# Attention pieces moved to a fixed table of FFN half slots, score steps in pairs, and another order of loads at the start

## The chip, the cores and the metric

The kernel runs on one core of a Trainium2 chip. The metric is the time of one execution on the device in microseconds (us). The engines are TensorE (PE in the profile), VectorE (DVE), ScalarE (ACT), GpSimd (POOL) and SyncE (SP), which here only issues transfers. Each engine works through its own queue in order and waits for others by semaphores.

## The reference, cut to what matters

Attention with a decay over 8 batches of 8 heads, 576 positions, 64 columns; its output x is normalised and goes through a gated FFN (512 to 1536 to 512) over all 4608 rows:

```python
scores = scale * q @ k.T;  cum = cumsum(log(clip(f, 1e-4, 1)))
attn = softmax(where(causal, -1e9, scores + cum[:, None] - cum[None, :]))
x = (attn @ v)                        # -> 4608 x 512, rows by batch and position
xn = x / sqrt(mean(x * x) + 1e-6) * rms_g
out = (silu(xn @ w_gate) * (xn @ w_val)) @ w_out
```

## The kernel before, in words

**Attention.** A batch has four pairs of heads, p = 0 to 3. For a pair, `cast` (L169) brings q and k to bf16; `transposes` (L192) turns the nine 128 x 128 blocks of q and k in two parts through the one PSUM bank `tr`, and VectorE copies each part to QK (L202). `scores` (L241) makes three steps, bank 0 to 2, each in a buffer `bg`; ScalarE takes the exponential of 128 x 1024 (L248) and GpSimd sets the masked triangle to zero (L216). `scores4` (L221) is the small step for the last 64 keys, in the bank `po`. `values` (L266), once a head, multiplies with the scaled v (`scale_v`, L177, on GpSimd), and VectorE divides by the row sums into x (L277, L278). `po` is one bank, so each head waits until the x of the head before it is out.

**Between.** `squares` (L288), `root` (L294, L296, GpSimd), `normed` (L305) and `transpose_x` (L307) make the normalised x and turn it, again through `tr`, to xT (L318). The rows of one batch lie in two FFN groups, since a batch has 576 rows and a group 512.

**FFN.** Nine groups. A group has 32 half slots h: 0 to 23 are `gate` (even) and `value` (odd) of the 12 chunks of 128 columns, 24 to 31 the two halves of the four projections. A gate takes a `bg` buffer; ScalarE makes a tanh of it (L387), VectorE combines (L388), the value goes to the other half of the same buffer, and VectorE makes hT (L396). A projection's result is copied out by ScalarE to `ores` (L411). `bg` has three buffers, shared by gates, projections and score steps, handed out in turn: each waits for the last reader of the third buffer before it.

**The order.** Every engine's order is that in which the program calls these functions. Batch 0 goes first, alone (L436 to L459). From batch 1 on the pieces of attention form a list of steps (`attention`, `finish`, `first`), and `knots` (L470) spreads the list evenly over the half slots, so that batch g + 1 ends within group g. Transfers of q, k and v are issued on SP's queue, those of batch 0's v and of the weights on GpSimd's.

Of the kernel before, what the change touches and what calls it, by code (L numbers as in the profile page):

```python
# [9 lines left out]
BF16 = mybir.dt.bfloat16  # L10
# [12 lines left out]
def kernel(  # L23
# [30 lines left out]
    qkt = ctx.enter_context(tc.tile_pool(name="qkt", bufs=2))  # L54
# [31 lines left out]
    def load_pair(n, what="qkv"):  # L86

        b, h0, i = n // NP, 2 * (n % NP), n % NST
        for name, src, dst in (("q", q, q32[i]), ("k", k, k32[i]), ("v", v, v32[i])):
            for h in range(2 * (name in what)):  # L90
                eng = nc.gpsimd if name == "v" and b == 0 else nc.sync
                eng.dma_start(out=dst[:, h, :, :], in_=src[b, h0 + h, 0:512, :].rearrange("(j p) d -> p j d", p=128))  # L92

    def load_last(b, what="qkv"):
        for name, src, dst in (("q", q, r32[b % 2][0:64, :, :]), ("k", k, r32[b % 2][64:128, :, :]), ("v", v, s32[b % 2])):
            if name in what:
                eng = nc.gpsimd if name == "v" and b == 0 else nc.sync
# [209 lines left out]
    def transpose_x(b, dc):  # L307
        xn = xns[b]
        tp = ps_tr.tile([128, NB * 128], BF16, name="tr")
        for j in range(NB):  # L310
            nc.tensor.transpose(tp[:, j * 128:(j + 1) * 128], xn[:, j, dc * 128:(dc + 1) * 128], ident)  # L311
        t0 = b * S
        while t0 < (b + 1) * S:
            g = t0 // GT
            t1 = min((g + 1) * GT, (b + 1) * S)
            if g not in xTs:
                xTs[g] = xtp.tile([128, NDC, GT], BF16, name="xT")
            nc.vector.tensor_scalar_mul(xTs[g][:, dc, t0 - g * GT:t1 - g * GT],  # L318
                                        tp[:, t0 - b * S:t1 - b * S], rg[:, dc:dc + 1])
            t0 = t1  # L320

    def attention(b):


        def tr(p, part):
            return lambda: transposes(b, p, part)

        def sc(p, bank):
            return lambda: scores(b, p, bank)

        def val(h):
            return lambda: values(b, h)

        def ahead(p):
            return lambda: (cast(b, p), scale_v(b, p)) if p < NP else None

        a = []
        for p in range(NP):
            a += [[tr(p + 1, 0)] if p + 1 < NP else [],
                  [sc(p, 0)],  # L340
                  [val(2 * p - 2), ahead(p + 2)] if p else [ahead(2)],
                  [tr(p + 1, 1)] if p + 1 < NP else [],
                  [sc(p, 1)],
                  [val(2 * p - 1)] if p else [],
                  [lambda p=p: scores4(b, p)],
                  [sc(p, 2)],
                  []]
        return a

    def finish(b):  # L350

        def sq(*js):
            return [lambda j=j: squares(b, j) for j in js]

        def xn(*js):
            return [lambda j=j: normed(b, j) for j in js]

        def x(dc):
            return [lambda: transpose_x(b, dc)]

        return {2: [lambda: values(b, 6)], 5: [lambda: values(b, 7)], 6: sq(0, 1), 7: sq(2, 3),
                8: sq(4) + [lambda: root(b)], 10: xn(0, 1), 11: xn(2, 3), 12: xn(4),
                14: x(0), 16: x(1), 18: x(2), 20: x(3)}

    def first(b):

        return {0: [lambda: (cast(b, 0), scale_v(b, 0))], 3: [lambda: (cast(b, 1), scale_v(b, 1))],
                5: [lambda: transposes(b, 0, 0)], 8: [lambda: transposes(b, 0, 1)]}
# [54 lines left out]
    def merged(*parts):  # L423

        n = max(at + (max(p) + 1 if isinstance(p, dict) else len(p)) for at, p in parts)
        a = [[] for _ in range(n)]
        for at, p in parts:
            for i, work in (p.items() if isinstance(p, dict) else enumerate(p)):
                a[at + i] += work
        return a  # L430

    def run(works):
        for work in works:
            work()

    def order():  # L436
# [33 lines left out]
        knots = [(0, 0), (2, 0)] + [(per * g, 9 + n * g + 21) for g in range(1, B)]  # L470
        assert knots[-1][1] == len(stream), (knots, len(stream))
        i = 0
        for h, work in enumerate(ffn):
            if h == 4:
# [3 lines left out]
            for (h0, i0), (h1, i1) in zip(knots, knots[1:]):
                if h0 <= h < h1:
                    want = i0 + (i1 - i0) * (h - h0) / (h1 - h0)  # L480
                    while i < want:
                        run(stream[i])
                        i += 1
            if h >= knots[-1][0]:
                while i < len(stream):
                    run(stream[i])
                    i += 1
            work()
# [34 lines left out]
```

## Time and profile before

| | us |
|---|---|
| median of two timed runs | 470.27 (470.17 to 470.38) |
| profiled execution | 470.79, span 468.8 |
| TensorE busy | 400.8 (85%) |
| VectorE, ScalarE, GpSimd busy | 262.3, 214.1, 179.1 |
| mean granted TensorE clock | 0.97 of 2.4 GHz |
| first FFN group's first matmul | 58.2 after the span's start |
| first group; five equal groups; group 6; group 7 | 64.25; 48.13 each; 39.72; 31.08 |

Times of rows are counted from the span's start. A matmul's end is modelled and overlaps the next one, so the distance from one start to the next tells more than a listed duration. An idle time stands in brackets with what ended it.

### The profile page before, as it was taken

The numbers are of one execution on the slowest core, as the hardware profiler recorded it, in microseconds if no ns is written. First come the engines' busy times: TensorE is split into PE (matmuls) and PEld (weight loads), VectorE is DVE, ScalarE is ACT, GpSimd is POOL, SyncE is SP. The second block draws the span as 40 slices with busy tenths as digits, with TensorE's granted clock in tenths as the row PEclk, the third lists the DMA queues.
The fourth block names the chain that finished last, engine by engine and source line by source line (L and its number), as shares of the span: only waits on it lengthen the run. The fifth ranks groups of instructions, "written<-read, shape, count | busy, mean of one in ns | idle before, by whom it ended". The sixth has DMA issues, their size and how long they took to land.

```text
span 468.8 us, 8739 instructions
## 1 busy us (share of the span) xinstructions
PE 400.8 (85%) x3317; PEld 201.1 (43%) x3317; DVE 262.3 (56%) x544; ACT 214.1 (46%) x354; POOL 179.1 (38%) x362
## 2 busy tenths in 40 slices
PE   0385398986999899989998999899989998999996
PEld 0153144543444444444444544444444444444442
DVE  1742565734575646674766377627762775572670
ACT  1354226654547435644554455535563543332321
POOL 6383718665173517351735173516451111000000
PEclk9996589998999999999999999999999999999999
DMA  9999498993173416431553146320001000101002
GB/s 159 210 200 204 107 179 146 181 199 96 45 156 83 110 48 138 102 92 67 128 111 90 68 107 130 75 85 2 2 24 45 24 1 28 62 1 69 22 1 89
DMA packets 120298, 43.19 MB, mean 92 GB/s; under 512 B 110688, under 2 KB 115296, under 8 KB 120256
## 3 DMA queue, kind: packets, MB, share of 16 engines
q1 hardware_dynamic: 115088, 36.73, 34.8%
q0 software_dynamic: 5168, 5.90, 7.5%
q8 instruction: 26, 0.43, 0.4%
q14 instruction: 16, 0.13, 0.1%
HBM read 37.90 MB, written 9.44 MB: 101 GB/s over the span
## 4 chain that ended last, share of the span: by engine, by line
PE 63%; DVE 17%; ACT 6%; POOL 4%; issue 4%; SPq 3%; DMA 2%; POOLq 0%; DVEq 0%; ACTq 0%
PE bg L384 16%; PE bg L405 16%; PE bg L394 15%; PE po L274 5%; PE bg L212 4%; DVE xn L305 4%; DVE th L388 3%; DVE x L278 3%; SPq L92 3%; ACT th L387 3%; DVE hT L396 2%; PE tr L311 2%; PE tr L200 2%; ACT junk L288 2%; DVE QK L202 2%
## 5 line engine op out<-in xcount | busy, mean ns | idle before, releaser
L388 DVE SCALAR_TENSOR_TENSOR th<-th,bg 128x512 f32<-128x512 f32 x108 | 74.2, 687 | 81.6 <-ACT th L387 81.4
L248 ACT ACTIVATE PT<-bg 128x1024 bf16<-128x1024 f32 x96 | 97.8, 1022 | 47.7 <-PE bg L212 47.3
L387 ACT ACTIVATE th<-bg 128x512 f32<-128x512 f32 x108 | 64.4, 596 | 106.1 <-PE bg L384 103.7
L384 PE MATMUL bg<-xT,wg 128*128 128x512 bf16 x432 | 112.2, 383 | 0.0
L394 PE MATMUL bg<-xT,wv 128*128 128x512 bf16 x432 | 112.1, 382 | 0.0
L405 PE MATMUL bg<-wo,hT 128*128 128x512 bf16 x432 | 102.3, 383 | 2.0 <-DVE hT L396 2.0
L216 POOL TENSOR_SCALAR_AFFINE_SELECT PT<-PT 128x256 bf16<-128x256 bf16 (+1 forms) x96 | 47.6, 495 | 92.3 <-ACT PT L248 91.2
L396 DVE SCALAR_TENSOR_TENSOR hT<-th,bg 128x512 bf16<-128x512 f32 x108 | 74.0, 685 | 10.3 <-PE bg L394 2.3
L405 PEld LDWEIGHTS <-hT 128*128 128x128 bf16 x432 | 39.9, 98 | 46.8 <-issue 3.6
L394 PEld LDWEIGHTS <-wv 128*128 128x128 bf16 x432 | 38.2, 98 | 42.9 <-issue 5.9
L384 PEld LDWEIGHTS <-wg 128*128 128x128 bf16 x432 | 37.8, 99 | 37.2 <-issue 1.4
L200 PE MATMUL tr<-ident,qkb 128*128 128x128 bf16 x288 | 28.8, 229 | 28.7 <-DVE QK L202 8.2
L318 DVE TENSOR_SCALAR xT<-tr,rg 128x512 bf16<-128x512 bf16 (+7 forms) x64 | 20.6, 363 | 56.3 <-PE tr L311 56.3
L411 ACT COPY ores<-bg 128x512 f32<-128x512 f32 x36 | 21.1, 585 | 55.0 <-PE bg L405 55.0
L274 PEld LDWEIGHTS <-PT 128*128 128x128 bf16 x896 | 36.6, 101 | 18.9 <-POOL PT L216 6.0
L212 PE MATMUL bg<-QK 64*128 64x64 bf16 (+3 forms) x576 | 39.9, 247 | 0.0
L200 PEld LDWEIGHTS <-qkb 128*128 128x128 bf16 x288 | 21.1, 102 | 41.6 <-issue 16.6
L202 DVE COPY QK<-tr 128x640 bf16<-128x640 bf16 x64 | 28.9, 451 | 10.9 <-PE tr L200 10.9
L311 PE MATMUL tr<-ident,xn 128*128 128x128 bf16 x160 | 16.3, 233 | 20.4 <-DVE QK L202 12.0
L278 DVE TENSOR_TENSOR x<-po,rden 128x320 f32<-128x320 f32 x64 | 31.5, 492 | 2.4 <-DVE rden L277 0.2
L212 PEld LDWEIGHTS <-QK 64*128 64x128 bf16 x576 | 17.0, 97 | 28.3 <-issue 24.3
L274 PE MATMUL po<-Vs_119,PT 128*128 128x65 bf16 x448 | 22.2, 204 | 5.1 <-POOL PT L216 3.7
(105 smaller groups left out, 296.0 us busy)
## 6 DMA issues: line engine op xcount, KB each, us to landing
out_dram<-ores SPq DMA_DIRECT2D x36, 256.0 KB, 2.0
q_0_103<-in_q_dram SPq DMA_DIRECT2D x16, 128.0 KB, 2.9
k_0_107<-in_k_dram SPq DMA_DIRECT2D x16, 128.0 KB, 3.3
q_1_104<-in_q_dram SPq DMA_DIRECT2D x16, 128.0 KB, 3.4
k_1_108<-in_k_dram SPq DMA_DIRECT2D x16, 128.0 KB, 3.5
q_2_105<-in_q_dram SPq DMA_DIRECT2D x16, 128.0 KB, 3.0
k_2_109<-in_k_dram SPq DMA_DIRECT2D x16, 128.0 KB, 3.6
q_3_106<-in_q_dram SPq DMA_DIRECT2D x16, 128.0 KB, 2.7
```

The lines of the kernel that those rows point to most:

```text
L200: nc.tensor.transpose(tp[:, (c - c0) * 128:(c - c0 + 1) * 128], src[:, c, :, :].rearrange("p h d -> p (h d)"), ident)
L212: nc.tensor.matmul(sc[:, par, c:c + n], lhsT=QK[b, p][rows, KEYS[kj]:KEYS[kj] + 128], rhs=QK[b, p][rows, q0:q0 + n], start=True, stop=True)
L216: nc.gpsimd.affine_select(out=d, in_=d, pattern=pattern, compare_op=ALU.is_ge, fill=0.0, base=0, channel_multiplier=-1)
L248: nc.scalar.activation(t, sc, ACT.Exp, scale=scale)
L274: nc.tensor.matmul(po[:, qi, :], lhsT=weights_of(b, h, qi, kj), rhs=Vs[b % 2][:, kj, h, :], start=(kj == 0), stop=(kj == qi))
L278: nc.vector.tensor_tensor(xs[b][:, :, h * D:(h + 1) * D], po[:, :, 0:D], bcast(r[:, :], D), ALU.mult)
L384: nc.tensor.matmul(pg, lhsT=wg[:, dc, fc * 128:(fc + 1) * 128], rhs=xTs[g][:, dc, :], start=(dc == 0), stop=(dc == NDC - 1))
L387: readers[g, fc] = (nc.scalar.activation(t, pg, ACT.Tanh, scale=0.5), nc.vector.scalar_tensor_tensor(t, in0=t, scalar=1.0, in1=pg, op0=ALU ...
L388: nc.vector.scalar_tensor_tensor(t, in0=t, scalar=1.0, in1=pg, op0=ALU.add, op1=ALU.mult))
L394: beside(nc.tensor.matmul(pv, lhsT=wv[:, dc, fc * 128:(fc + 1) * 128], rhs=xTs[g][:, dc, :], start=(dc == 0), stop=(dc == NDC - 1)), reade ...
L396: nc.vector.scalar_tensor_tensor(hT, in0=ths.pop((g, fc)), scalar=0.5, in1=pv, op0=ALU.mult, op1=ALU.mult)
L405: beside(nc.tensor.matmul(po, lhsT=hTs[g, fc][:, j * 128:(j + 1) * 128], rhs=wo[:, fc, :], start=(fc == 0), stop=(fc == NFC - 1)), readers ...
```

## The change

Batch 0: k and its last rows (r) go by the Pool queue, v by SP; the pieces of the four pairs stand in another order, the value step one pair behind; x is turned into two idle `bg` buffers, all four parts, and then copied out by VectorE and ScalarE in turn. QK has three buffers instead of two. The ones column of V goes from VectorE to GpSimd. From batch 1 on a table says which piece stands ahead of which half slot of a group, the same in each: `ALL1` for batch 1 beside group 0; `ONE`, a block with no FFN between, ahead of group 1; `LAST` (second half of batch g + 1) and `FIRST` (first half of batch g + 2) beside groups 1 to 8. A piece is a letter and its arguments: C cast and scale_v, T transposes, S scores, L scores4, V values, Q squares, R root, N normed, X transpose_x. Two score steps mostly stand together.

```diff
-    qkt = ctx.enter_context(tc.tile_pool(name="qkt", bufs=2))
+    qkt = ctx.enter_context(tc.tile_pool(name="qkt", bufs=3))
...
-    load_pair(0, "qk")
-    load_last(0, "qk")
-    load_pair(0, "v")
-    load_pair(1, "qk")
-    load_last(0, "v")
-    load_pair(1, "v")
-    load_pair(2)
-    load_pair(3)
+    for n in range(NP):
+        load_pair(n, "q")
+        load_pair(n, "k", nc.gpsimd)
+        if n == 0:
+            load_last(0, "q")
+            load_last(0, "k", nc.gpsimd)
+        load_pair(n, "v")
+        if n == 0:
+            load_last(0, "v")
...
-        for b in range(2):
-            nc.vector.tensor_copy(Vs[b][:, :, :, D], decT[:, :, b * H:(b + 1) * H])
+        nc.gpsimd.tensor_copy(Vs[0][:, :, :, D], decT[:, :, 0:H])
...
-    def transpose_x(b, dc):
-        xn = xns[b]
-        tp = ps_tr.tile([128, NB * 128], BF16, name="tr")
+    def turn_x(b, dc, tp):
         for j in range(NB):
-            nc.tensor.transpose(tp[:, j * 128:(j + 1) * 128], xn[:, j, dc * 128:(dc + 1) * 128], ident)
+            nc.tensor.transpose(tp[:, j * 128:(j + 1) * 128], xns[b][:, j, dc * 128:(dc + 1) * 128], ident)
+
+    def put_x(b, dc, tp, on_act=False):
+
         t0 = b * S
         while t0 < (b + 1) * S:
             g = t0 // GT
             t1 = min((g + 1) * GT, (b + 1) * S)
             if g not in xTs:
                 xTs[g] = xtp.tile([128, NDC, GT], BF16, name="xT")
-            nc.vector.tensor_scalar_mul(xTs[g][:, dc, t0 - g * GT:t1 - g * GT],
-                                        tp[:, t0 - b * S:t1 - b * S], rg[:, dc:dc + 1])
+            dst, src = xTs[g][:, dc, t0 - g * GT:t1 - g * GT], tp[:, t0 - b * S:t1 - b * S]
+            if on_act:
+                nc.scalar.mul(dst, src, rg[:, dc:dc + 1])
+            else:
+                nc.vector.tensor_scalar_mul(dst, src, rg[:, dc:dc + 1])
             t0 = t1
 
...
+    LAST = {2: "S22 S30", 4: "L2", 6: "V4", 8: "S31 S32 V5", 10: "L3", 12: "V6", 14: "V7", 15: "Q0", 16: "Q1",
...
+    FIRST = {2: "T00", 5: "T01", 11: "C1", 14: "S00 S01", 16: "T10", 17: "C2", 18: "T11", 20: "S02 S10 T20",
...
+    ALL1 = {2: "C1", 3: "T00", 4: "T01", 6: "C2", 7: "S00 S01 T10", 8: "T11", 10: "C3", 11: "S02 S10", 12: "L0 T20",
...
+    ONE = ("1N0 1N1 1N2 1N3 1N4 2T00 2T01 2S00 2S01 2T10 2T11 2S02 2S10 1X0 2L0 2T20 1X1 2S11 2S12 2V0 1X2 2T21 2V1 2L1 "
...
+        for p in range(NP):
+            scores(0, p, 0)
+            if p > 0:
+                scores4(0, p - 1)
+            if p + 1 < NP:
+                cast(0, p + 1)
+                transposes(0, p + 1, 0)
+            scores(0, p, 1)
+            if p + 1 < NP:
+                scale_v(0, p + 1)
+            if p > 0:
+                values(0, 2 * p - 2)
+            if p + 1 < NP:
+                transposes(0, p + 1, 1)
+            scores(0, p, 2)
+            if p > 0:
+                values(0, 2 * p - 1)
+            if p == 1:
+                load_last(1)
+            if p == 2:
+                load_w(0)
+        scores4(0, 3)
         values(0, 6)
         values(0, 7)
+        load_w(1)
         for j in range(NB):
             squares(0, j, nc.vector if j % 2 else None)
         root(0)
         for j in range(NB):
             normed(0, j, on_act=j % 2 == 1)
+        banks = [ps_b.tile([128, 2, 1024], BF16, name="bg") for _ in range(2)]
         for dc in range(NDC):
-            transpose_x(0, dc)
-
-        n = 9 * NP
-        parts = [(0, first(1))]
-        for b in range(1, B):
-            at = 9 + n * (b - 1)
-            parts += [(at, attention(b)), (at + n, finish(b))]
-            if b + 1 < B:
-                parts.append((at + n - 9, first(b + 1)))
-        stream = merged(*parts)
+            turn_x(0, dc, banks[dc // 2][:, dc % 2, :])
+        for dc in range(NDC):
+            put_x(0, dc, banks[dc // 2][:, dc % 2, :], on_act=dc % 2 == 1)
+        piece(1, "C0")
...
+            if g == 0:
+                for what in ALL1.get(h, "").split():
+                    piece(1, what)
+                if h in (16, 22, 27):
+                    piece(2, {16: "C0", 22: "C1", 27: "C2"}[h])
+            else:
+                if g == 1 and h == 0:
+                    for what in ONE.split():
+                        piece(int(what[0]), what[1:])
+                        if what == "2S10":
+                            piece(2, "C3")
+                for what in LAST.get(h, "").split():
+                    piece(g + 1, what)
+                for what in FIRST.get(h, "").split():
+                    piece(g + 2, what)
+                for what in NEXT.get(h, "").split():
+                    piece(g + 3, what)
+                if g == 1 and h == 0:
+                    piece(3, "C0")
             work()
```

In the order of the engines this shows at three places. First the start: SP's queue before, from its first transfer on (q_0 and k_0 are pair 0, r_0 the last 64 rows of q and k, v and s the same of v):

```order
L101 DMA fr<-in_f_dram 64x576
L92 DMA q_0_103<-in_q_dram 128x4x64 x2
L92 DMA k_0_107<-in_k_dram 128x4x64 x2
L98 DMA r_0_115<-in_q_dram 64x8x64
L98 DMA r_0_115<-in_k_dram 64x8x64
L92 DMA q_1_104<-in_q_dram 128x4x64 x2
```

and POOL's queue now, from its first transfer on:

```order
L91 DMA k_0_107<-in_k_dram 128x4x64
masks.py:199 ISA
masks.py:199 AFFINE_SELECT ident_f<-ident_f 128x128
L91 DMA k_0_107<-in_k_dram 128x4x64
L96 DMA r_0_115<-in_k_dram 64x8x64
L91 DMA k_1_108<-in_k_dram 128x4x64 x2
```

The k part of r moved from SP's fifth group of transfers to Pool's third transfer, where s of v stood before.

Second, VectorE at the end of batch 1. Before, beside the projections of group 0 (QK is the copy of turned q and k, xn the normalised x, xT its turned copy, rden and x the end of a value step):

```order
L202 COPY QK<-tr 128x640
L396 SCALAR_TENSOR_TENSOR hT<-th,bg 128x512
L277 RECIPROCAL rden<-po 128x5
L278 TENSOR_TENSOR x<-po,rden 128x5x64
L202 COPY QK<-tr 128x512
L277 RECIPROCAL rden<-po 128x5
L278 TENSOR_TENSOR x<-po,rden 128x5x64
L202 COPY QK<-tr 128x640
L305 TENSOR_SCALAR xn<-x,rs 128x512 x4
```

and now, in the block ahead of group 1:

```order
L275 RECIPROCAL rden<-po 128x5
L276 TENSOR_TENSOR x<-po,rden 128x5x64
L303 TENSOR_SCALAR xn<-x,rs 128x512 x5
L200 COPY QK<-tr 128x640
L200 COPY QK<-tr 128x512
L200 COPY QK<-tr 128x640
L200 COPY QK<-tr 128x512
L321 TENSOR_SCALAR xT<-tr,rg 128x448
L321 TENSOR_SCALAR xT<-tr,rg 128x128
```

The five xn stand ahead of the first of four QK copies in a row; before, QK copies stood between the steps that lead up to them.

Third, ScalarE in a steady group. Before (th is the tanh of a gate, PT the exponential of a score step, PT_0 to PT_2 those of the small step):

```order
L387 ACTIVATE th<-bg 128x512
L248 ACTIVATE PT<-bg 128x1024
L387 ACTIVATE th<-bg 128x512
L228 ACTIVATE PT_1_122<-po 128x2x64
L248 ACTIVATE PT<-bg 128x1024
L387 ACTIVATE th<-bg 128x512 x2
```

and now, from a group's first gate on:

```order
L346 ACTIVATE th<-bg 128x512
L246 ACTIVATE PT<-bg 128x1024 x2
L346 ACTIVATE th<-bg 128x512
L226 ACTIVATE PT_2_123<-po 128x2x64
L346 ACTIVATE th<-bg 128x512 x2
L246 ACTIVATE PT<-bg 128x1024 x2
```

One exponential between two tanh became two, with more tanh between the pairs.

## Rows read from the trace of the kernel before

**Rows 1.** Busy time of each engine by stage: start:end, length, busy (instructions), clock, DMA share.

```profile
0.00:16.00 16.00, 1.20 (x9) 0.94 (x9) 5.24 (x19) 2.67 (x3) 7.86 (x18) 1.00 1.02 174
...
58.20:122.45 64.25, 54.87 (x516) 28.05 (x515) 33.45 (x74) 32.03 (x51) 34.33 (x72) 0.94 0.78 151
...
170.58:218.72 48.14, 44.41 (x398) 22.31 (x396) 29.15 (x63) 24.86 (x42) 21.43 (x44) 1.00 0.40 97
...
363.12:402.84 39.72, 37.93 (x280) 18.21 (x279) 24.38 (x49) 17.46 (x33) 4.44 (x9) 1.00 0.08 28
402.84:433.92 31.08, 31.08 (x145) 14.07 (x144) 17.14 (x26) 9.31 (x16) 0.00 (x0) 1.00 0.09 35
```

**Rows 2.** Timeline of the start: start, duration, engine, line, operation, count [idle before].

```profile
3.50 0.70 POOL L98 DMA_DIRECT2D s_0_117<-in_v_dram  x1
...
11.81 0.23 DVE L174 CAST qkb<-r_0_115 128x128 bf16<-128x128 f32 x1 [4.99 <-DMA r_0_115<-in_k_dram]
...
18.31 0.49 DVE L161 COPY decT<-po 128x320 f32<-128x320 f32 x1 [1.60 <-PE po L160]
...
22.21 1.02 ACT L248 ACTIVATE PT<-bg 128x1024 bf16<-128x1024 f32 x1 [4.84 <-PE bg L212]
```

**Rows 3.** Transfers by issuing line: queue, count, size, median us from issue to landing.

```profile
wv<-in_moe_w_val_dram POOLq DMA_DIRECT2D x3, 512.0 KB, 10.6
...
s_0_117<-in_v_dram POOLq DMA_DIRECT2D x1, 128.0 KB, 5.7
```

**Rows 4.** Timeline of batch 0's pairs and its end.

```profile
30.89 0.61 PE L212 MATMUL bg<-QK 64*128 64x64 bf16 x10
...
47.33 0.49 DVE L278 TENSOR_TENSOR x<-po,rden 128x320 f32<-128x320 f32 x1
...
56.23 0.71 PE L311 MATMUL tr<-ident,xn 128*128 128x128 bf16 x5 [0.74 <-DVE xT L318]
...
58.19 1.91 PE L384 MATMUL bg<-xT,wg 128*128 128x512 bf16 x4
```

**Rows 5.** Timeline of TensorE in a steady group.

```profile
174.49 1.03 PE L394 MATMUL bg<-xT,wv 128*128 128x512 bf16 x4
175.44 0.40 PE L212 MATMUL bg<-QK 64*128 64x64 bf16 x10
175.78 1.04 PE L384 MATMUL bg<-xT,wg 128*128 128x512 bf16 x4
...
182.28 0.59 PE L274 MATMUL po<-Vs_120,PT 128*128 128x65 bf16 x14
...
182.74 0.44 PE L200 MATMUL tr<-ident,qkb 128*128 128x128 bf16 x5
```

**Rows 6.** Timelines of VectorE and ScalarE in the same group.

```profile
174.96 0.69 DVE L388 SCALAR_TENSOR_TENSOR th<-th,bg 128x512 f32<-128x512 f32 x1 [0.59 <-ACT th L387]
175.75 0.69 DVE L396 SCALAR_TENSOR_TENSOR hT<-th,bg 128x512 bf16<-128x512 f32 x1
...
196.93 0.62 ACT L288 ACTIVATE junk<-x 128x512 bf16<-128x512 f32 x1
...
197.67 0.63 ACT L288 ACTIVATE junk<-x 128x512 bf16<-128x512 f32 x1
...
198.30 1.00 ACT L248 ACTIVATE PT<-bg 128x1024 bf16<-128x1024 f32 x1
199.21 0.59 ACT L387 ACTIVATE th<-bg 128x512 f32<-128x512 f32 x1
...
213.46 0.58 ACT L411 COPY ores<-bg 128x512 f32<-128x512 f32 x1 [1.67 <-PE bg L405]
```

**Rows 7.** Timelines at the end of the first group.

```profile
108.98 2.17 DVE L305 TENSOR_SCALAR xn<-x,rs 128x512 bf16<-128x512 f32 x4 [3.98 <-POOL rs L296]
...
112.56 0.44 PE L311 MATMUL tr<-ident,xn 128*128 128x128 bf16 x5 [2.94 <-DVE QK L202]
```

**Rows 8.** Busy time by stretch, behind that wait.

```profile
114.00:116.00 2.00, 2.00 (x7) 0.79 (x6) 0.31 (x1) 0.00 (x0) 0.00 (x0) 0.50 0.80 180
```

More of the change, by code (lines that the diff above doesn't have):

```diff
@@ L84, with load_pair @@
     QB = [consts.tile([128, 128], BF16, name=f"QB_{i}") for i in range(3)]
-    def load_pair(n, what="qkv"):
+    def load_pair(n, what="qkv", eng=nc.sync):
         b, h0, i = n // NP, 2 * (n % NP), n % NST
@@ L178, in scale_v @@
         n, h0 = b * NP + p, 2 * p
-        if b > 1 and p == 0:
+        if b > 0 and p == 0:
             nc.gpsimd.tensor_copy(Vs[b % 2][:, :, :, D], decT[:, :, b * H:(b + 1) * H])
@@ L317, in transpose_x @@
                 xTs[g] = xtp.tile([128, NDC, GT], BF16, name="xT")
-            nc.vector.tensor_scalar_mul(xTs[g][:, dc, t0 - g * GT:t1 - g * GT],
-                                        tp[:, t0 - b * S:t1 - b * S], rg[:, dc:dc + 1])
-            t0 = t1
[L322 to L368, printed above, removed]
+            dst, src = xTs[g][:, dc, t0 - g * GT:t1 - g * GT], tp[:, t0 - b * S:t1 - b * S]
[3 more added lines that the diff above has]
+                nc.vector.tensor_scalar_mul(dst, src, rg[:, dc:dc + 1])
+            t0 = t1
+    def transpose_x(b, dc):
+        tp = ps_tr.tile([128, NB * 128], BF16, name="tr")
+        turn_x(b, dc, tp)
+        put_x(b, dc, tp)
     hTs = {}
@@ L420, with piece @@
             ffn += [lambda g=g, j=j: project(g, j, 0), lambda g=g, j=j: project(g, j, 1)]
[L423 to L434, printed above, removed]
+    def piece(b, what):
+        kind, args = what[0], [int(c) for c in what[1:]]
+        if not 0 <= b < B:
+            return
+        if kind == "C":
+            cast(b, *args)
+            scale_v(b, *args)
+        elif kind == "N":
+            normed(b, *args)
+        else:
+            {"T": transposes, "S": scores, "L": scores4, "V": values, "Q": squares, "R": root,
+             "X": transpose_x}[kind](b, *args)
+    LAST = {2: "S22 S30", 4: "L2", 6: "V4", 8: "S31 S32 V5", 10: "L3", 12: "V6", 14: "V7", 15: "Q0", 16: "Q1",
+            17: "Q2", 18: "Q3", 19: "Q4 R", 21: "N0", 22: "N1", 23: "N2", 24: "N3", 25: "N4", 26: "X0", 27: "X1",
+            29: "X2", 31: "X3"}
+    FIRST = {2: "T00", 5: "T01", 11: "C1", 14: "S00 S01", 16: "T10", 17: "C2", 18: "T11", 20: "S02 S10 T20",
+             22: "L0", 23: "T21 C3", 24: "V0", 26: "S11 S12 V1", 28: "L1 T30", 29: "V2", 30: "S20 S21 V3 T31"}
+    NEXT = {28: "C0"}
+    ALL1 = {2: "C1", 3: "T00", 4: "T01", 6: "C2", 7: "S00 S01 T10", 8: "T11", 10: "C3", 11: "S02 S10", 12: "L0 T20",
+            14: "S11 S12 V0", 15: "T21", 16: "V1", 17: "L1", 18: "S20 S21 V2", 19: "T30", 20: "V3", 21: "T31",
+            22: "L2", 23: "S22 S30", 25: "S31 S32 V4", 27: "V5", 28: "L3", 29: "V6", 30: "V7",
+            31: "Q0 Q1 Q2 Q3 Q4 R"}
+    ONE = ("1N0 1N1 1N2 1N3 1N4 2T00 2T01 2S00 2S01 2T10 2T11 2S02 2S10 1X0 2L0 2T20 1X1 2S11 2S12 2V0 1X2 2T21 2V1 2L1 "
+           "1X3 2S20 2S21 2V2 2T30 2V3 2T31")
     def order():
@@ L470, in order @@
[L470 to L474, printed above, removed]
+            turn_x(0, dc, banks[dc // 2][:, dc % 2, :])
+        for dc in range(NDC):
+            put_x(0, dc, banks[dc // 2][:, dc % 2, :], on_act=dc % 2 == 1)
+        piece(1, "C0")
+        per = 2 * (NFC + 4)
+        for i, work in enumerate(ffn):
+            g, h = i // per, i % per
+            if i == 2:
@@ L475, in order @@
                 load_w(2)
-            if h == 10:
+            if i == 9:
                 load_wo()
[L478 to L487, printed above, removed]
+            if g == 0:
[3 more added lines that the diff above has]
+                    piece(2, {16: "C0", 22: "C1", 27: "C2"}[h])
+            else:
+                if g == 1 and h == 0:
[11 more added lines that the diff above has]
+                    piece(3, "C0")
```

11 lines of the change are left out of this document (1 added, 10 removed).

## The prediction

> **What bounds the kernel now.** I read the busy time of each engine by stage first, since TensorE is the busiest in every FFN stage [rows 1], then the timelines of each stage for what TensorE waits for. In rows 1 a group of the FFN alone takes 31.08 us (144 matmuls, 0.216 each: 0.86 for a gate or value half slot, 1.30 for half a projection). Each of five equal groups, with one batch of attention beside it, takes 48.1; the first takes 64.25, the one with the end of batch 7 39.72. TensorE's first FFN matmul starts the first of these stages, at 58.2. So the span is 58.2 + 64.25 + 5 x 48.13 + 39.72 + 65.96 (two bare groups and the last transfer) = 468.8, and the change touches every term but the last. The profiled run took 470.79; the two timed runs have a median of 470.27, 0.5 less.
>
> **The start.** The first cast of batch 0 waits until 11.81 for the k part of tile r [rows 2], the fifth transfer group on SP. Now that part stands third in the Pool queue, where s stood: issued at 3.50 [rows 2], landed a median 5.7 later [rows 3], so 9.2, and 2.6 us come off. Bounds: 0 (the same 16 engines carry it all) and 5 (k could land with q). I take 2.6, since s had the same bytes ahead of it. The page DMA: Bandwidth & Descriptors of the Trainium skill (Rules for kernel authors) says that spreading transfers over queues wins no bandwidth, only issue time; by that the 2.6 would be 0, and no run here shows it yet.
>
> The first score step stood behind the cast and turn of pair 1, so the first exponential ran at 22.21. Now only the decay columns precede it: their copy at 18.31 [rows 2], less 2.6, gives 15.7, and 0.54 of scores and the handover make 16.4; so 5.8 earlier. From there to the last x (47.33 + 0.49 [rows 4]) the old loop took 25.6 for four pairs. At the lower clock a pair costs TensorE three score steps of 0.54, turns of about 0.64 and 0.54 [rows 4], two value steps of 1.0 (about twice their later 0.44) and one small step of 0.2 = 5.0; with about 0.9 of waits (the x of one head must be out of the bank before the next) I find the same 25.6 and take no gain there.
>
> In the tail x was turned through one bank, each of three turns waiting 0.74 for VectorE's copy [rows 4]. Two idle FFN banks take that wait away: 2.2. ScalarE's two copies end before the gate's last matmul needs them. First gate: 58.2 - 5.8 - 2.2 = **50.2**. The weights come in time: the first pair is asked for in pair 2's work, near 32 by this count, and lands up to 10.6 later [rows 3]; the second, asked for after the last value step near 42, is first read by the fifth gate, past 60.
>
> **A steady group.** Attention beside it costs TensorE 4 x (turns 0.28 + 0.23, three score steps of 0.33, 0.07, two value steps of 0.44) + 4 turns of x of 0.28 = 10.9 (a listed duration ends about 0.16 after the next may start) [rows 5]. Work: 42.0, so the old group loses 6.1. What the table loses, I follow by its queues. From a gate's end to its hT's end: 0.21 to the tanh, 0.63 to the first VectorE step, 0.79 to the second, 0.69 for it = 2.3 [rows 6]. A gate takes the buffer of the third last bg tile. After a pair of score steps that is the gate before, whose value (0.86) and the pair (0.66) cover 1.5 to 1.9. So the gates at half slots 2, 8, 14 and 20 wait 0.57, 0.41, 0.41 and 0.67. In the last, the five squares also stand ahead of the tanh (0.63 to 0.75 each). The third projection and the next group's first gate take a buffer whose last reader is the copy to ores, just issued: 0.21 + 0.58 + 0.05 [rows 6], less 0.35 of pieces in the first case: 0.49 and 0.85. The first turn of x waits 0.85 for the last xn, one turn 0.13. Sum 4.4. The other gates' waits are covered: each has a buffer freed two half slots earlier.
>
> A score step alone costs 0.33 and a seam ahead: the value before it takes 0.95 instead of 0.86 [rows 5]. A pair has one seam; some fall into the waits, and I charge 0.2. Group: 42.0 + 4.4 + 0.2 = **46.6**, 1.5 less, five times 7.7. The page TensorEngine Tiling (Array Packing) of the skill (Key Properties) says that a change of tiling mode drains the engine, with which the 0.09 agrees; charging all six seams by it would make 46.9.
>
> Group 6 has only batch 7's rest: 31.1 + 4.3 + waits 1.8 + 0.2 = **37.4**, 2.3 less.
>
> **The first group and the block behind it.** Here the change costs. The old 64.25 held batch 1, its x and more than half of batch 2, spread out. Now batch 1 alone lies in the first group: 31.1 + 9.8, waits of the same kinds 5.9 (eight waits of 0.2 to 0.95; the second turn, two gates and the first projection carry 3.1), 1.8 for the lower clock at the start (the old first gate took 1.91 [rows 4]): 48.6. Then xn, x and half of batch 2 run with no FFN between. Batch 1's squares start only with the last half projection. Five of 0.75 [rows 6], of which 1.2 lie beside it, the root 1.5 and five xn of 0.54 [rows 7] end 6.8 after the projection. VectorE has them ahead of its first QK copy, so TensorE gets one turn done and stands. Then eleven turns go through the one transposing bank, each with its copy about 1.1 at full clock: 12; the waits for x between value steps add 2. Together 20.7. At the lower clock turns, scores and values on this path cost about 6.5 more: 27. The old kernel shows the clock after a hole: a wait of 2.94 before 112.56 [rows 7] is followed by a granted clock of 0.50 at 114 to 116 [rows 8], that is 1.2 of 2.4 GHz. The new hole is twice as long and TensorE half idle behind it, so I take 25.8, near the slow end. First group and block: **74.4**, 10.2 more than before.
>
> **Sum.** 50.2 + 74.4 + 233.0 + 37.4 + 66.0 = 461.0 for 468.8; 7.8 off 470.79 and the 0.5: **462.5**.
>
> **Costed at nothing.** The ones column of V on GpSimd instead of VectorE lies beside pair 0's exponentials; without that cover it costs its 0.4. The third QK buffer only removes waits. GpSimd is busy 21.4 of 48.1 in a group [rows 1], so its masks and casts come in time; bunched four deep they would delay a value step by about 1.
>
> **Rivals.**
> 1. The clock stays up. If the start is dense enough to be granted 2.4 GHz early, and the block too, the block costs 20.7 and the loop at the start gives 2: 462.5 - 5.1 - 2 = 455.4. For: the pairs at the start leave TensorE about 0.9 idle in 5.9. Against: the old hole [rows 7, 8]. Chance 0.22.
> 2. The steady groups win nothing. With every queued step at its listed length (exponential 1.00, tanh 0.59, VectorE 0.69) instead of start to start (0.91, 0.47, 0.60), the same walk makes 48.0 a group: 469.5. Chance 0.14.
> 3. The Pool queue brings k no sooner: +2.6, 465.1. All queues share the 16 engines, whose share is 1.02 in the first 16 us [rows 1], so k waits among the same bytes. Against: s landed by 9.2 in that crowd. The Trainium skill's page named above states this as its rule. Chance 0.09.
> 4. Slower: ScalarE becomes the bound behind the paired score steps. Two exponentials (2 x 0.91) stand ahead of the next tanh. The walk has that tanh needed only three buffers later. If the gate that waits is one whose own tanh is behind the pair, each such place costs 1.83 per group. One place per group makes 472; two make 481, slower by over 2%. It decides from 48.2 us a group on, where the other gains are used up. For: six such pairs stand at fixed places in each group, where the old order had one exponential at a time. Against: ScalarE is busy 24.9 of 48.1 [rows 1]. Chance 0.07.
>
> **Numbers.** My forecast has 0.48, with 457 to 467 as its own range (block 20.7 to 27, group 45.9 to 47.4, start 0 to 5). Range of all: 453 to 470; it leaves out the slower rival and the tails. Two per cent, about what a measurement of this kernel can tell from no change, is 9.4 us: 460.9 and 479.7. Faster: rival 1 and the lower part of my own (0.48 x 0.42), 0.42. Slower: 0.05. Within: 0.53.
>
> **What would show it.** The first exponential near 16.4 and the r cast near 9.2; the first gate near 50; in the profile by stage the hole of about 6 us before batch 1's xn, with the clock at 0.50 behind it; gates behind pairs waiting for hT, and the first gate of each group for ores; groups of 46 to 47. A steady group over 48, or a block of 30, would make the forecast wrong; a clock of 1.00 through the block would make it too high.

## The result, and the profile after

The changed kernel takes 442.19 us (two runs, 440.19 and 444.19) for 470.27: a ratio of 0.940 (0.922 to 0.959). Timed again in more rounds, it took 442.12, 442.49, 443.90 and 444.88, ratio 0.943 (0.941 to 0.945); a fifth run, which took 591 at a mean granted clock of 0.66, is left out. The median of these four, 443.2, is what the experiments are held against. The forecast was 462.5, with 453 as its low end: wrong, the time lies below the range.

Busy time by stage, as in [rows 1], of the profiled run of 444.19 (span 442.5): start, first group, the block, a stretch of the block, a steady group, group 6.

```profile
14.00:47.66 33.66, 21.18 (x248) 14.40 (x249) 17.21 (x41) 16.89 (x26) 21.91 (x40) 0.78 1.20 202
47.66:92.66 45.00, 42.72 (x374) 21.78 (x380) 24.92 (x50) 24.41 (x40) 27.54 (x55) 0.98 1.13 203
92.66:117.98 25.32, 15.03 (x164) 10.62 (x163) 10.14 (x28) 10.60 (x17) 10.48 (x25) 0.60 0.26 72
98.00:100.00 2.00, 0.71 (x6) 0.44 (x7) 1.14 (x3) 0.00 (x0) 0.46 (x2) 0.50 0.00 0
206.35:250.63 44.28, 42.50 (x390) 22.91 (x396) 28.63 (x61) 25.10 (x42) 21.34 (x44) 1.00 0.42 105
339.57:376.35 36.78, 35.46 (x249) 17.72 (x254) 23.10 (x45) 17.09 (x32) 3.82 (x8) 1.00 0.08 30
```

Stage by stage, from the first gate of each group:

| stage | before | forecast | after | error |
|---|---|---|---|---|
| start, to the first gate | 58.2 | 50.2 | 47.7 | -2.5 |
| first group | 64.25 (with half of batch 2) | 48.6 | 45.0 | -3.6 |
| block | none | 25.8 | 25.3 | -0.5 |
| five steady groups | 240.7 | 233.0 | 221.6 | -11.4 |
| group 6 | 39.7 | 37.4 | 36.8 | -0.6 |
| rest | 66.0 | 66.0 | 66.1 | +0.1 |

The errors add to 18.5, which is the whole difference between 461.0 and 442.5, the spans forecast and profiled. Five steady groups carry 11.4 of it. The waits of TensorE in one of them, before (four waits) and after (one row, four waits); columns are total, times, longest. Before, 170.42 to 218.56:

```profile
PE tr L311 <- DVE QK L202: 1.8, 1, 1.8
PE tr L200 <- DVE xT L318: 0.8, 1, 0.8
PE tr L200 <- DVE QK L202: 0.7, 1, 0.7
PE bg L405 <- DVE hT L396: 0.2, 1, 0.2
```

After, 206.35 to 250.63:

```profile
PE bg L343 <- DVE hT L355: 1.4, 4, 0.4
```

The turns no longer stand in line; the gates behind the pairs wait for hT, at the four places forecast, but nobody waits for ores. A listed wait begins at the modelled end of the matmul before it, which reaches past the next possible start, so it is shorter than what is lost from start to start. TensorE at the fourth place, half slot 20:

```profile
225.89 0.44 PE L198 MATMUL tr<-ident,qkb 128*128 128x128 bf16 x5
226.17 1.03 PE L343 MATMUL bg<-xT,wg 128*128 128x512 bf16 x4
...
229.19 1.03 PE L353 MATMUL bg<-xT,wv 128*128 128x512 bf16 x4
230.15 0.62 PE L210 MATMUL bg<-QK 64*128 64x64 bf16 x12
230.70 0.45 PE L198 MATMUL tr<-ident,qkb 128*128 128x128 bf16 x5
231.56 1.02 PE L343 MATMUL bg<-xT,wg 128*128 128x512 bf16 x3 [0.40 <-DVE hT L355]
```

A turn of five blocks with no wait behind it takes 0.28 to the gate (225.89 to 226.17), here 0.86: the gate waits 0.58, of which 0.40 is listed. At half slots 2, 8 and 14 the same count gives 0.58, 0.40 and 0.39; in all that is 1.9 where the list has 1.35.

The end of that group and the start of the next show that nobody waits for ores. Timeline of TensorE and then of ScalarE (start, duration, idle time before in brackets), to be read with [rows 5, 6]:

```profile
249.34 1.46 PE L364 MATMUL bg<-wo,hT 128*128 128x512 bf16 x6
250.63 1.03 PE L343 MATMUL bg<-xT,wg 128*128 128x512 bf16 x3
```

```profile
247.12 1.95 ACT L246 ACTIVATE PT<-bg 128x1024 bf16<-128x1024 f32 x2
250.88 0.59 ACT L370 COPY ores<-bg 128x512 f32<-128x512 f32 x1 [1.81 <-issue]
```

The gate starts 1.29 after the projection's half, with no gap, and 0.25 before the copy to ores even begins. Of the three buffers one still waits for that copy, so the gate has one of the pair's, whose exponentials ran from 247.12 to 249.07.

The start in the same run, as in [rows 2, 4]: the r cast, the decay columns, then ScalarE's first exponential, then TensorE from the turns of x on.

```profile
9.01 0.23 DVE L172 CAST qkb<-r_0_115 128x128 bf16<-128x128 f32 x1 [2.19 <-DMA r_0_115<-in_k_dram]
...
15.51 0.49 DVE L160 COPY decT<-po 128x320 f32<-128x320 f32 x1 [1.60 <-PE po L159]
...
39.56 0.49 DVE L276 TENSOR_TENSOR x<-po,rden 128x320 f32<-128x320 f32 x1
```

```profile
15.95 1.02 ACT L246 ACTIVATE PT<-bg 128x1024 bf16<-128x1024 f32 x1 [1.38 <-PE bg L210]
```

```profile
44.80 0.83 PE L307 MATMUL bg<-ident,xn 128*128 128x128 bf16 x4 [5.51 <-DVE xn L303]
45.98 1.89 PE L307 MATMUL bg<-ident,xn 128*128 128x128 bf16 x16 [0.35 <-DVE xn L303]
47.66 2.19 PE L343 MATMUL bg<-xT,wg 128*128 128x512 bf16 x4
```

And the block's hole, which answers to [rows 7]: VectorE's xn, and behind them the QK copy on which TensorE waits for 5.79.

```profile
96.25 2.07 DVE L303 TENSOR_SCALAR xn<-x,rs 128x512 bf16<-128x512 f32 x5 [5.38 <-POOL rs L294]
98.23 0.48 DVE L200 COPY QK<-tr 128x640 bf16<-128x640 bf16 x1
```

```profile
98.77 0.58 PE L198 MATMUL tr<-ident,qkb 128*128 128x128 bf16 x4 [5.79 <-DVE QK L200]
```

### The profile page after: what moved, and what is told of

It is laid out like the page before. It is cut to its first block, busy times and chain, and to the rows that moved or that the text cites. A ratio compares the mean times of both kernels' runs of the same rounds, so it can differ in the third digit from the quotient of the medians.

```text
span 442.5 us, 8691 instructions
## 1 busy us (share of the span) xinstructions
PE 390.3 (88%) x3264; PEld 208.0 (47%) x3317; DVE 257.7 (58%) x538; ACT 217.0 (49%) x358; POOL 178.0 (40%) x364
## 4 chain that ended last, share of the span: by engine, by line
PE 78%; DVE 9%; ACT 5%; issue 4%; POOL 2%; DMA 1%; DVEq 0%; ACTq 0%; POOLq 0%
PE bg L364 20%; PE bg L343 19%; PE bg L353 18%; PE po L272 7%; PE bg L210 6%; PE tr L198 3%; DVE hT L355 3%; PE tr L307 2%; ACT PT L246 2%; DVE th L347 1%; DMA r_0_115<-in_k_dram 1%; ACT junk L286 1%; DVE x L276 1%; DVE QK L200 1%; ACT th L346 1%
## 5 line engine op out<-in xcount | busy, mean ns | idle before, releaser
L343 PE MATMUL bg<-xT,wg 128*128 128x512 bf16 x400 | 109.1, 381 | 10.3 <-DVE hT L355 8.4
L353 PE MATMUL bg<-xT,wv 128*128 128x512 bf16 x427 | 110.0, 379 | 0.3 <-issue 0.2
L246 ACT ACTIVATE PT<-bg 128x1024 bf16<-128x1024 f32 x96 | 93.6, 1022 | 33.3 <-PE bg L210 33.2
L364 PE MATMUL bg<-wo,hT 128*128 128x512 bf16 x416 | 99.0, 379 | 0.8
L353 PEld LDWEIGHTS <-wv 128*128 128x128 bf16 x432 | 41.4, 98 | 47.7 <-issue 1.2
L343 PEld LDWEIGHTS <-wg 128*128 128x128 bf16 x432 | 39.9, 98 | 47.7 <-issue 11.4
L210 PE MATMUL bg<-QK 64*128 64x64 bf16 (+3 forms) x576 | 35.4, 254 | 0.8 <-DVE QK L200 0.5
L200 DVE COPY QK<-tr 128x640 bf16<-128x640 bf16 x64 | 28.9, 451 | 11.4 <-PE tr L198 11.3
L321 DVE TENSOR_SCALAR xT<-tr,rg 128x448 bf16<-128x448 bf16 (+7 forms) x56 | 18.0, 363 | 23.8 <-PE tr L307 23.8
L275 DVE RECIPROCAL rden<-po 128x5 f32<-128x5 f32 x64 | 12.2, 190 | 32.0 <-PE po L272 32.0
L286 ACT ACTIVATE junk<-x 128x512 bf16<-128x512 f32 x38 | 23.9, 628 | 4.9 <-DVE x L276 4.4
```

Of the source, the lines that this page charges most:

```text
L210: nc.tensor.matmul(sc[:, par, c:c + n], lhsT=QK[b, p][rows, KEYS[kj]:KEYS[kj] + 128], rhs=QK[b, p][rows, q0:q0 + n], start=True, stop=True)
L246: nc.scalar.activation(t, sc, ACT.Exp, scale=scale)
L343: nc.tensor.matmul(pg, lhsT=wg[:, dc, fc * 128:(fc + 1) * 128], rhs=xTs[g][:, dc, :], start=(dc == 0), stop=(dc == NDC - 1))
L353: beside(nc.tensor.matmul(pv, lhsT=wv[:, dc, fc * 128:(fc + 1) * 128], rhs=xTs[g][:, dc, :], start=(dc == 0), stop=(dc == NDC - 1)), reade ...
L364: beside(nc.tensor.matmul(po, lhsT=hTs[g, fc][:, j * 128:(j + 1) * 128], rhs=wo[:, fc, :], start=(fc == 0), stop=(fc == NFC - 1)), readers ...
```

## The experiments

**The change again.** No edit.

> The changed kernel itself again, in more rounds. Theory (its time differs from run to run by when the clock rises in batch 0's pairs): 439 to 444, the first gate at 46 to 47.7, and from the second group on the same lengths to 0.05. Rival (the steady groups differ from run to run): groups from 44.0 to 45.

Measured: 442.1 to 444.9. The spread is seen best in the profiles of kernels that share its start: the first gate lies between 46.0 and 47.7, first group and block take 70.1 to 71.6, and a steady group 44.1 (the first) or 44.3, in some profiles one of them 0.35 more. The theory holds for the most part; one time lies 0.9 above its range.

**The parts by themselves.** First the old start before the new table, then the new start before the old stream.

```
-    for n in range(NP): load_pair(n, "q"); load_pair(n, "k", nc.gpsimd) ...
+    load_pair(0, "qk"); load_last(0, "qk"); load_pair(0, "v") ...   # as before the change
-        for p in range(NP): scores(0, p, 0) ...  x by two FFN banks
+        for i, works in enumerate(attention(0)): run(works) ...  x by ps_tr
```

> The start of the kernel before (its load order and queues, its order of batch 0, x turned through the one transposing bank, ones columns by VectorE), and from the first gate on the table of the change. Theory (the parts add): the start is worth the 10.5 us by which the first gate came earlier (47.66 for 58.19), so 442.2 + 10.5 = 452.7, first gate near 58.2, first group 45 and block 25. Rival (part of the start's gain is given back later, because the first group of the change waits for weights or runs at a lower clock that the later start would not have): 447 to 450, with a shorter first group.

Measured: 454.63, ratio 0.968 (0.967 to 0.970), 11.4 over 443.2. First gate at 57.4, first group and block 69.98, steady groups 44.29. The time lies 1.9 above the theory.

> The new start alone, with the evenly spread stream of the kernel before behind it. Theory (the parts add): 470.3 - 10.5 = 459.8; the steady groups keep 48.1 and the first group 64. Rival (the weights, which are asked for as early as before but read earlier, hold the first group): 462 to 466, with the first group 67 or more.

Measured: 458.16, ratio 0.975 (0.972 to 0.978). First gate at 47.3, first group 61.8, not 67: the weights hold nothing. Steady groups 48.14. The parts add: the start is worth 11 to 12, and all of the rest, some 15, belongs to the order of the groups. This kernel has the third QK buffer too, and its steady groups are as long as without it.

**The pairs.** Four of the six pairs of a group are opened.

```
-8: "S31 S32 V5"   20: "S02 S10 T20"   26: "S11 S12 V1"   30: "S20 S21 V3 T31"
+8: "S31 V5 S32"   20: "S02 T20 S10"   26: "S11 V1 S12"   30: "S20 V3 S21 T31"
```

> In the table, the two score steps of four of the six pairs of a group get a turn or a value step between them, in the same half slot; nothing else moves. Theory (a pair is cheaper than two single steps): in the steady groups of the changed kernel a pair takes 0.55 from its start to the next work and 0.09 ahead of it, together 0.64, and a single step of the kernel before 0.34 and 0.09, so two of them 0.86. With 4 x 5 + 1 = 21 pairs opened, 21 x 0.22 = 4.6 us more: 442.2 + 4.6 = 446.8, and a steady group of 45.2 instead of 44.3. Rival (the pairs themselves give nothing, only the places of the waits in the table do): 442 to 443, group 44.3 to 44.5.

Measured: 446.42, ratio 0.951 (0.949 to 0.952), 3.2 over 443.2; four steady groups of 44.71 to 44.97, one of 45.98. TensorE at half slot 30 of a steady group, first in this kernel and then after the change:

```profile
247.95 0.39 PE L210 MATMUL bg<-QK 64*128 64x512 bf16 x2
248.27 0.63 PE L272 MATMUL po<-Vs,PT 128*128 128x65 bf16 x15
248.84 0.40 PE L210 MATMUL bg<-QK 64*128 64x256 bf16 x6
249.16 0.40 PE L198 MATMUL tr<-ident,qkb 128*128 128x128 bf16 x4
```

```profile
246.53 0.61 PE L210 MATMUL bg<-QK 64*128 64x512 bf16 x8
...
247.54 0.39 PE L198 MATMUL tr<-ident,qkb 128*128 128x128 bf16 x4
```

From start to start the two steps and the value step take 1.21 opened and 1.01 as a pair: 0.20 for an opened pair, where the theory has 0.22. Four of them make 0.8, but the group grows by 0.43 only, because the hT waits fall by 0.4 in exchange. So the theory's price is about right and its sum too high; what else lies in the 3.2 (a first group and block of 71.6, that one group) was not separated.

Now pairs in the old stream, with nothing else changed.

```
-                  [sc(p, 1)],
+                  [sc(p, 1), sc(p, 2)],
...
-                  [sc(p, 2)],
+                  [],
```

> The kernel before, with the second and third score step of each pair of heads run together; nothing else is changed. Theory (a pair costs 0.22 less than two single steps wherever it stands): four pairs a batch for seven batches beside the FFN and batch 0, some 28 x 0.22 = 6 less: 464. Rival (in the old stream the gate behind a pair waits for a buffer, and the gain of the change is the table's): 469 to 472.

Measured: 454.19, ratio 0.966 (0.965 to 0.968): 10 us better than the theory. First gate 55.3, first group 61.7, steady groups 46.43 (1.70 less), group 6 39.1. Its waits in a steady group:

```profile
PE tr L311 <- DVE QK L202: 0.9, 1, 0.9
PE tr L200 <- DVE xT L318: 0.8, 1, 0.8
PE tr L200 <- DVE QK L202: 0.7, 1, 0.7
PE bg L212 <- DVE hT L396: 0.5, 1, 0.5
```

Four pairs at 0.22 are 0.9 of the 1.70; the wait of x's turn, 1.8 before, gives another 0.9, since the projection is less far ahead of VectorE: the copy that the turn waits for begins 5.48 after an hT in both kernels (206.10 and 244.26), the half projection ahead of the turn 3.61 after it instead of 2.68. A new wait of 0.5 for hT, 0.2 before, takes 0.3 back. At the start the loop of batch 0's pairs takes 23.0 instead of 25.6, although each of its value steps takes 1.0 there, the length at the lower clock. A step that is moved pays twice here, once on its own and once by the wait that it takes from another.

**Which buffer a gate takes.** Four pairs are put half a slot later, ahead of the value.

```
-LAST = {2: "S22 S30", ... 8: "S31 S32 V5"     FIRST: 14: "S00 S01"  20: "S02 S10 T20"
+LAST = {3: "S22 S30", ... 8: "V5", 9: "S31 S32"  FIRST: 15: "S00 S01"  20: "T20", 21: "S02 S10"
```

> The pairs of score steps that stand before the gates at half slots 2, 8, 14 and 20 stand one half slot later, before the values (four pairs in a group, two in group 6). Theory (a new tile of the FFN bank pool takes the buffer released first in the order of the program): the gate behind the value then takes the buffer of the pair's first step, whose exponential ends 1.5 after the pair begins, when 0.64 + 0.86 have gone by; the waits for hT, 1.35 in a steady group, go to 0.1 to 0.3, a group takes 43.1 to 43.3 and the kernel 442.2 - 5.5 x 1.1 = 436. Rival (the rule of the prediction, the buffer of the third last tile): the gate takes the buffer of the gate before, whose value ends just ahead of it, and waits 0.74 for its hT at each of four places, 3.0 a group for 1.35 now: 45.9 a group, 450.

Measured: 440.58, ratio 0.935 (0.933 to 0.938); steady groups 43.85, group 6 36.07. Timelines behind such a pair, TensorE, VectorE, ScalarE:

```profile
206.51 0.65 PE L210 MATMUL bg<-QK 64*128 64x64 bf16 x12
207.10 1.04 PE L353 MATMUL bg<-xT,wv 128*128 128x512 bf16 x4
...
208.18 1.02 PE L343 MATMUL bg<-xT,wg 128*128 128x512 bf16 x4
```

```profile
208.17 0.69 DVE L355 SCALAR_TENSOR_TENSOR hT<-th,bg 128x512 bf16<-128x512 f32 x1 [0.23 <-PE bg L353]
```

```profile
207.11 1.93 ACT L246 ACTIVATE PT<-bg 128x1024 bf16<-128x1024 f32 x2
```

The gate begins at 208.18, while VectorE is only beginning the hT of the gate before: it doesn't have that gate's buffer. The pair's second exponential runs until 209.04. So the gate has the buffer of the pair's first one, which ends near 208.1. This decides against the rule of the prediction. The same can be asked of all 108 gates in the trace: in the changed kernel the last reader that the prediction's rule names is still at work at the start of 7 gates, in this kernel at that of 24; the one that the theory names, at none. The size is short of the theory: 0.44 a group instead of 1.1, since new waits come in place of those for hT (start to start, 0.68 for an exponential at half slot 16 and 0.13 to 0.18 at the other three places; and a listed 0.3 for an xn).

**The start's pieces.** k by SP; x through the one bank; the second pair's turn ahead of the first score step.

```
-        load_pair(n, "k", nc.gpsimd)
+        load_pair(n, "k")
...
-            load_last(0, "k", nc.gpsimd)
+            load_last(0, "k")
```

> The k of batch 0 goes by SP's queue in the same place of the order, instead of the Pool queue. Theory (the term of the prediction): the first cast waits for r's k until 11.8 again, 2.6 later: 444.8. Rival (all queues share the 16 engines, so the queue wins nothing): 442 to 442.5, r cast at 9 to 10.

Measured: 443.22, ratio 0.940 (0.935 to 0.944): nothing. The r cast comes even earlier:

```profile
8.31 0.23 DVE L172 CAST qkb<-r 128x128 bf16<-128x128 f32 x1 [2.81 <-DMA r<-in_k_dram]
```

r's k is issued at 4.38 here, as before the change at 4.40, in the same place of SP's queue. What differs from the kernel before is that v and s of batch 0, issued on the Pool queue from 1.39 on there, are issued behind r's k, from 5.06 on. So the 2.8 us by which the cast came sooner in the changed kernel do not come from k's queue; what is left is the transfers that stood beside k (the changed kernel issues them from 3.29 on). No run puts those alone back. The page DMA: Bandwidth & Descriptors of the Trainium skill (Rules for kernel authors) has it that spreading transfers over issuing engines wins no bandwidth; the times with k by SP and by the Pool queue, 443.22 and 443.2, agree.

```
-        banks = [ps_b.tile([128, 2, 1024], BF16, name="bg") for _ in range(2)] ...
+        for dc in range(NDC): transpose_x(0, dc)
```

> Batch 0's x is turned through the one transposing bank, one copy after each turn, all by VectorE, as before the change. Theory (the term of the prediction): three waits of 0.74 come back, 2.2 us: 444.4. Rival (the gate then waits for the weights anyway, or the copies at the end are as long as before): 442 to 443.

Measured: 446.33, ratio 0.949 (0.947 to 0.951), 3.1 over 443.2. TensorE at the end of the start:

```profile
47.36 0.71 PE L307 MATMUL tr<-ident,xn 128*128 128x128 bf16 x5 [0.74 <-DVE xT L321]
...
50.26 0.71 PE L307 MATMUL tr<-ident,xn 128*128 128x128 bf16 x5 [0.74 <-DVE xT L321]
51.20 1.06 PE L343 MATMUL bg<-xT,wg 128*128 128x512 bf16 x2 [0.22 <-issue]
```

The three waits of 0.74 are back, 2.2 of the 3.1; the turns themselves run at the lower clock either way. The other 0.9 was not taken apart.

```
+        cast(0, 1); transposes(0, 1, 0); transposes(0, 1, 1)
         for p in range(NP): scores(0, p, 0) ...
```

> The changed kernel with the cast and the two turns of batch 0's second pair ahead of the first score step again, as before the change; loads and the rest of the start as changed. Theory (the prediction: the first exponential then comes 3.2 later, and the loop behind it keeps its length): 442.2 + 3.2 = 445.4. Rival (the pair that is turned ahead is missing from the loop, which ends as early): 442 to 443.

Measured: 446.08, ratio 0.949 (0.947 to 0.951), 2.9 over 443.2; the first exponential at 19.02, 3.07 later. The time is the theory's, but the loop does not keep its length: it takes 21.8 for 24.1, as the rival has it in part, and the first gate comes at 48.4, only 0.8 later than in the profile after the change. The loop of this profile has the higher clock for 6.8 us instead of 3.4; against the changed start with the clock up as long (46.5 and 46.7) the gate comes 1.7 to 1.9 later. The rest of the 2.9 lies behind the first gate (0.6 in first group and block, 0.8 in the first steady group of the profiled run) and was not separated.

**The block.** First the turns into the hole, then the whole block into the projections.

```
-ONE = ("1N0 1N1 1N2 1N3 1N4 2T00 2T01 2S00 2S01 2T10 2T11 2S02 ...
+ONE = ("2T00 2T01 2S00 2S01 2T10 2T11 1N0 1N1 1N2 1N3 1N4 2S02 ...
```

> In the block between the first and the second group, the four turns and the first two score steps of batch 2 are put ahead of the five xn of batch 1, where they stood behind them, so that VectorE copies QK while ScalarE still squares. Theory (the hole of 5.79 us in which TensorE waits for a QK copy queued behind xn is the block's largest loss): the hole goes, the block falls from 25.3 to about 19, and the time to 436; if the clock then also stays at 1.00 through the block, to 431. Rival (the block is bound by the chain squares, root, xn, x turned one at a time through the one bank, and the work moved ahead only fills a wait that comes back before the first turn of x): 440 to 442.

Measured: 437.83, ratio 0.932 (0.931 to 0.933), 5.4 less than 443.2. Busy time of the block in this kernel:

```profile
91.00:111.75 20.75, 14.57 (x162) 9.95 (x160) 10.80 (x28) 10.52 (x17) 11.23 (x26) 0.59 0.45 117
```

The hole is gone, and the block takes 20.75 for 25.32, where 19 was expected; but the clock is not up: 0.59 over the block for 0.60.

```
 ALL1: batch 1 ends at half slot 23 (was 30); 24: "Q0 D1 Q2 D3 Q4 R"   # D: square on VectorE
+ONE1 = {28: "N0 N1 N2 N3 N4", 29: "X0", 30: "X1", 31: "X2"}           # batch 1
+ONE = {..., 24: "T00", 25: "T01", 26: "S00 S01 T10", 27: "T11", 28: "C3 S02 S10", ...}  # batch 2
+END = "1X3 2T21 2V1 2L1 2S20 2S21 2V2 2T30 2V3 2T31"
```

> Batch 1 is packed into the 24 gate and value half slots of the first group, and the block that stood between the first two groups (end of batch 1, first half of batch 2) is spread over the eight half projections, but for a short rest; two of batch 1's squares go to VectorE. Theory (the block is slow because nothing covers its one transposing bank, its copies and the chain to xn, and because the clock falls in it): 31.1 of FFN, 9.8 of batch 1, about 7.8 of the block at full clock (turns 2.0 and 1.1, scores 2.6, values 1.9, small 0.2), 1.8 for the clock at the start and 6 to 8 of waits make 57 to 59 for first group and block instead of 70.3: 429 to 431. Rival (ScalarE's exponentials and VectorE's copies cannot follow batch 1 at that density, so the first group grows by what the block loses): 436 to 442.

Measured: 434.53, ratio 0.924 (0.921 to 0.926). First group and block, then TensorE's longest waits in it:

```profile
46.74:108.25 61.51, 51.77 (x531) 28.02 (x540) 36.09 (x82) 33.53 (x52) 37.82 (x77) 0.98 0.95 182
```

```profile
PE po L224 <- DVE x L276: 3.7, 4, 1.6
PE tr L198 <- DVE QK L200: 1.9, 2, 1.2
```

61.5 for 70.3, the clock at 0.98. That is 3 more than the theory's 58, so the time lies above its 431; the largest waits are those of the small score step (L224), which needs the bank whose x is just being written. So the last kernel moves those steps apart, and takes the pairs before values too.

```
-11: "V1 L1", 12: "S20 S21 T30"   END = "1X3 2T21 2V1 2L1 2S20 2S21 2V2 2T30 2V3 2T31"
+11: "V1", 12: "L1 S20 S21 T30"   END = "1X3 2V1 2T21 2L1 2S20 2S21 2T30 2V2"   # T31, V3 in group 1
```

> The two orders that won, together: the block spread over the half projections, and the pairs before values. Besides, the small score steps stand a step further behind the value step whose bank they reuse, and the last turn and value step of the block lie in the second group's first two half slots. Theory (the gains add): 434.5 - 1.7 for the pairs - 1 to 2 for the waits of the small step (3.7 in all in the kernel with the spread block) = 431 to 432. Rival (the first group is bound by ScalarE and VectorE and takes back what the moved steps give): 433 to 434.

Measured: **429.38**, ratio 0.913 (0.911 to 0.915), the fastest of all and below both expectations: first group and block 58.74, steady groups 43.84. In the first group of this kernel and of the one before it, one gate begins while the last reader that the order of release names is at work (here 76.99, the hT ends at 77.48; it waits for an exponential instead). So that order is not the whole rule, and what is missing stays open.

## Why the prediction was wrong

**The step that failed** is the count of waits in a steady group, "Sum 4.4", and in it the sentence "A gate takes the buffer of the third last bg tile". (The description of the kernel before has the same rule, buffers "handed out in turn".) At the places in question a new tile takes the buffer that was released first, in the order of the program. A projection's tile stays in use over four half slots; the pair placed between is released before it, so the third projection and the next group's first gate find the pair's buffers, and the 0.49 and 0.85 charged for ores are 0. The first turn of x, charged 0.85 for the last xn, loses 0.17: it takes 0.55 to the next pair, 0.28 for itself and 0.10 for the seam ahead of the pair. One turn waits 0.22 for 0.13. The waits for hT were forecast well, since there both rules name the same buffer: 0.58, 0.40, 0.39 and 0.58 from start to start at half slots 2, 8, 14 and 20, where 0.57, 0.41, 0.41 and 0.67 were charged. Found in all: 2.3 for 4.4. The work, 44.28 less 2.3, is 42.0 for 42.2, and the group came out at 44.3 for 46.6. Of the 2.3 by which the group is off, the wrong buffer is 1.34 and the turn of x 0.68.

The first group was charged 5.9 of waits; 1.7 are listed, and its own sum leaves 2.3 (45.0 less 42.7). Its charges stand on the same walk, but which of them fell away was not taken apart. With group 6 and the five steady groups that is 15.6 of the 18.5. That the buffer is another than assumed was shown by the gate that begins while its predecessor's hT does; that the two charges for ores fall away by that rule alone was read from the trace after, and not tried one by one, and why the last xn came sooner than the walk had it stays open.

**Where the 3.84 a group come from.** Pairs in the old stream give 1.70. From its 46.43 on, listed waits fall from 2.9 to 1.4 and two more pairs at 0.22 make 0.4: together 1.9 of the other 2.14.

**The seam.** I took a single score step at 0.33 and charged 0.2 for the seams of all six pairs. From start to start the value step ahead of a pair takes 0.96 instead of 0.86 (229.19 to 230.15), so six seams make 0.6; but a pair takes 0.55 (230.15 to 230.70) and not twice 0.33. The two errors nearly cancel: 3.9 a group for 4.2. The page TensorEngine Tiling (Array Packing) of the Trainium skill (Key Properties) says that a change of tiling mode drains the engine. The trace agrees, with these 0.10; the six seams of 0.09 that I did not charge were nearer than my 0.2.

**The start.** The r cast was due at 9.2 and came at 9.01, but for another reason than its queue. The first exponential came at 15.95 for 16.4, and the order of the turn behind it is worth 3.07 at the first exponential, 3.2 forecast; of that the loop gives back over 1 by the first gate, so that the 2.9 in time lies so near the 3.2 is in part luck. The loop, given no gain, took 24.1 for 25.6; the tail gave 2.8 for 2.2, and 3.1 when undone. In both profiles the clock's records show 2.4 GHz for 3.4 us within the loop, so these 1.5 us belong to the order; where it is up for 10.2 us, as in the profile of the kernel with the turns moved ahead, the loop takes 22.65.

**The block** was right: a hole of 5.79 for "about 6", the clock at 0.50 behind it, 25.3 for 25.8. So was the rest, 66.1 for 66.0. The terms costed at nothing were not tried by themselves, but for the third QK buffer, which gives nothing in the old stream (48.14 a group).

**Rivals.** The first asked for the clock to stay up: in the block it did not, and in the loop for 3.4 us in the profiled run. The second had the steady groups win nothing: the reverse. The third is half right: the queue wins nothing, but the start came sooner. The fourth: ScalarE is busy 25.1 of 44.3, and in the steady group no gate behind a pair waited longer than 0.58, where 1.83 was the price.

## What to carry to other kernels

Before charging a wait for a buffer, find out in what order the pool gives its buffers back, and test the rule on a gap, or a missing one, in the trace at hand: the wrong rule charged 1.34 us a group here that nobody waits for, 6.7 over five groups. Count waits from start to start: the list showed 1.35 where 1.9 was lost. Run steps of another matmul shape together, and look also at whom they kept waiting. Work with a long chain and one bank (norm, turn, copy) belongs beside the dense matmuls, not between two groups of them: there it cost its time and the clock too.

## What was not expected of the hardware

The clock fell in the block even with its hole filled: in the kernel with the turns moved ahead, TensorE is busy 3.18 of 5.00 and the clock reads 0.87 over the first five microseconds, then 0.50 until the FFN begins, though it is busy 4.69 of 5.75 at the end.

```profile
91.00:96.00 5.00, 3.18 (x39) 1.67 (x35) 2.56 (x6) 4.76 (x10) 2.80 (x6) 0.87 1.02 276
...
106.00:111.75 5.75, 4.69 (x53) 3.65 (x55) 2.73 (x8) 2.22 (x3) 2.38 (x7) 0.50 0.00 0
```

With projections in between it reads 0.98. And the clock's column is not to be trusted at the start. In the trace of the changed kernel the clock's records begin with its first rise, at 29.1; ahead of it the column reads 1.00 with nothing behind it. A value step takes 0.95 there; in a steady group at 1.00 it takes 0.58.

```profile
20.00:25.00 5.00, 4.68 (x60) 3.35 (x58) 3.28 (x8) 3.65 (x5) 4.68 (x10) 1.00 1.31 210
```

```profile
23.68 0.95 PE L272 MATMUL po<-Vs_119,PT 128*128 128x65 bf16 x14
...
213.31 0.58 PE L272 MATMUL po<-Vs_119,PT 128*128 128x65 bf16 x14
```

There the durations tell the clock, and the column doesn't; the mean of 0.97 before the change is too high for the same reason. When it rises in batch 0's pairs, and for how long, differs from run to run, and with it the first gate: 46.0 to 46.3 where the records show it up for 10.2 us, 47.3 to 47.7 where for 3.4.
